# z on VectorE, earlier query normalizing, LN2 sums from accumulators and 640-wide evacuations in a gated mix of linear attention and a mixer MLP

## The chip, the cores and the metric

One Trainium2 chip, one of its cores. The metric is the device time of one execution in microseconds (us). The kernel before takes 268.58 us, median of the 4 runs timed beside the changed kernel (268.53 to 268.66). The profile's span, first to last instruction, is about 1.6 us shorter than that time: 267.0 us.

## The reference, cut to what matters

S = 2048 tokens, D = 640, 32 heads of 20, F = 1728, everything bf16.

```python
g = sigmoid((x * gate_w).sum(-1))
# A: linear attention
q, k, v = split(x @ wqkv); pq, pk = phi(q), phi(k)     # phi: t+1 if t>0 else exp(t); + 1e-6
kv  = einsum("bhsd,bhse->bhde", pk, v)
z   = pk.sum over tokens                               # [heads, 20] = 640 numbers
num = einsum("bhqd,bhde->bhqe", pq, kv)
den = einsum("bhqd,bhd->bhq", pq, z) + 1e-6
a   = (num / den) @ wo
# B: mixer
h   = gelu(layernorm(x) @ w1); hs = shift_by_quarter(h) @ w2
x1  = x + hs
b   = x1 + gelu(layernorm(x1) @ w3) @ w4
return g * a + (1 - g) * b
```

Of the kernel before, what the change touches and what calls it, by code (L numbers as in the profile page):

```python
# [50 lines left out]
class _Sched:  # L51
# [179 lines left out]
    def simulate(self):  # L231
        SEM_LAT = 60.0
        seq = self.seq
        while self.sim_pos < len(seq):
# [7 lines left out]
            if sem is not None and sem.startswith("d:") and nbytes < 0:  # L242
                self.eng_free[eng] = t + 1350.0
                end = t + 2800.0
                self.ev_time[(sem, val)] = end
            elif sem is not None and sem.startswith("d:"):
                self.eng_free[eng] = t + (500.0 if eng == "sp" else 1000.0)
                self.dma_free = max(self.dma_free, t) + nbytes / 330.0
                end = self.dma_free + 1900.0
                if self.ev_time.get((sem, val), 0.0) < end:  # L250
                    self.ev_time[(sem, val)] = end
            else:
                end = t + cost
                self.eng_free[eng] = end
                self.ev_time[(sem, val)] = end
# [169 lines left out]
def _build(nc, A_x, A_wqkv, A_wo, B_w1, B_w2, B_w3, B_w4, gate_w, out, dbg=None, stop=None):  # L425
# [55 lines left out]
    bn2 = pa.alloc("bn2", [128, NT, 2], F32)  # L481
    bns = pa.alloc("bns", [128, 4, 12], F32)
# [17 lines left out]
    zacc = pa.alloc("zacc", [128, D], F32)  # L500
# [12 lines left out]
    qprod = rb.alloc("qprod", [128, D], F32)  # L513
# [124 lines left out]
    def stt(out_ap, in0, scalar, in1, op0, op1):  # L638
        rd = [in0, in1] + ([scalar] if not isinstance(scalar, (int, float)) else [])
        n = nfree(out_ap)  # L640
        cost = (65.0 + n / 0.96) if (in_psum(in0) or in_psum(in1)) else (160.0 + 1.04 * n)
        return dve(lambda e: e.scalar_tensor_tensor(out_ap, in0, scalar, in1, op0, op1), rd, [out_ap], cost=cost)  # L642
# [81 lines left out]
    memset(pool, zacc[:], 0.0)  # L724
# [63 lines left out]
    def z_add(t):  # L788
        tt(pool, zacc[:, :] if t < NT - 1 else zsum[:, :], zacc[:, :], pk_tok[:, t, :], ALU.add)

    def ln_chunk_stats1(c):
        cs = slice(4 * c, 4 * c + 4)
        rs = lr[:, cs, 0:1].rearrange("p t o -> p (t o)")
        ts(pool, st1[:, 2, cs], rs, 1.0 / D, 0.0, ALU.mult, ALU.add)
        ts(pool, st1[:, 3, cs], st1[:, 1, cs], 1.0 / D, EPS_LN, ALU.mult, ALU.add)
        tt(pool, st1[:, 4, cs], st1[:, 2, cs], st1[:, 2, cs], ALU.mult)
        tt(pool, st1[:, 5, cs], st1[:, 3, cs], st1[:, 4, cs], ALU.subtract)
        tt(pool, st1[:, 6, cs], st1[:, 5, cs], negh[:, 0:4], ALU.pow)
        tt(pool, st1[:, 7, cs], st1[:, 2, cs], st1[:, 6, cs], ALU.mult)
        ts(pool, st1[:, 7, cs], st1[:, 7, cs], -1.0, 0.0, ALU.mult, ALU.add)  # L800
# [83 lines left out]
    def stats1(c):  # L884
        ln_chunk_stats1(c)
# [11 lines left out]
    for u in range(NT):  # L897
        IT.add("Z", ("z", u), 0.0, lambda u=u: z_add(u), deps=[(("n1", NT - 1), 0.0)] if u == 0 else [(("z", u - 1), 1.5)])
# [65 lines left out]
    for h in range(2):  # L964
# [3 lines left out]
    IT.add("KVF", ("zb",), 0.3, zb_group, deps=[(("z", NT - 1), 1.7)])  # L968
# [12 lines left out]
    def ln_chunk_stats2(c):  # L981
        cs = slice(4 * c, 4 * c + 4)
        mean = bn2[:, cs, 0:1].rearrange("p t o -> p (t o)")
        var = bn2[:, cs, 1:2].rearrange("p t o -> p (t o)")
        ts(pool, st2[:, 2, cs], var, 1.0, EPS_LN, ALU.mult, ALU.add)
        tt(pool, st2[:, 6, cs], st2[:, 2, cs], negh[:, 0:4], ALU.pow)
        tt(pool, st2[:, 7, cs], mean, st2[:, 6, cs], ALU.mult)
        ts(pool, st2[:, 7, cs], st2[:, 7, cs], -1.0, 0.0, ALU.mult, ALU.add)

    def w2_tile(t):  # L990
        tok = slice(2 + 128 * t, 2 + 128 * (t + 1))
        b1, b2 = bank(), bank()
        mm_group(ps[:, b1, 0:512], [(hsT[:, k, tok], w2[:, k, 0:512]) for k in range(KD)])
        mm_group(ps[:, b2, 0:128], [(hsT[:, k, tok], w2[:, k, 512:D]) for k in range(KD)])
        tt(dve, x_tok[:, t, 0:512], ps[:, b1, 0:512], x_tok[:, t, 0:512], ALU.add)
        tt(dve, x_tok[:, t, 512:D], ps[:, b2, 0:128], x_tok[:, t, 512:D], ALU.add)
        sb_ = slot("bns", 4)
        dve(lambda e: e.bn_stats(bns[:, sb_, 0:6], x_tok[:, t, 0:320]), [x_tok[:, t, 0:320]], [bns[:, sb_, 0:6]], cost=400.0)
        dve(lambda e: e.bn_stats(bns[:, sb_, 6:12], x_tok[:, t, 320:D]), [x_tok[:, t, 320:D]], [bns[:, sb_, 6:12]], cost=400.0)
        dve(lambda e: e.bn_aggr(bn2[:, t, :], bns[:, sb_, :]), [bns[:, sb_, :]], [bn2[:, t, :]], cost=110.0)  # L1000
        if t % 4 == 3:
            ln_chunk_stats2(t // 4)
# [43 lines left out]
    def a_tile(t):  # L1046
# [13 lines left out]
    def w4_half(t):  # L1060
# [21 lines left out]
    def w4_tile(t):  # L1082
# [20 lines left out]
        stt(x_tok[:, t, 0:512], ps[:, b1, 0:512], stg[:, 3, t:t + 1], abx[:, sa, 0:512], ALU.mult, ALU.add)  # L1103
        stt(x_tok[:, t, 512:D], ps[:, b2, 0:128], stg[:, 3, t:t + 1], abx[:, sa, 512:D], ALU.mult, ALU.add)
# [20 lines left out]
    for t in range(NT):  # L1125
# [95 lines left out]
```

## The kernel before: the parts that the change touches

The kernel is made by a small order-maker. Every piece of work is an item of a stream with dependencies; the order-maker keeps a model of each engine's time and always emits the item whose inputs it believes to be ready first. The emitted order is then fixed: on the chip each engine runs its list in order and waits on semaphores.

```python
# _Items.run(), cut: the choice of the next item
for d, lag in it["deps"]:
    if d not in done: ok = False; break
    v = done[d] + 100.0                       # modelled end of the dependency
    if v > est: est = v
key = (max(est, t_pe), 0 if it["dur"] == 0.0 else 1, -cp[n])
if best is None or key < best[0]: best = (key, n, s_)
```

The work runs in stages: q and k projections with phi (10 to 54 us in the profile), G = x^T pk (54 to 82), mixed with w1; then w1 and w2 (to 119), w3, and from 149 on `a` (normalized query times M), w3 and w4 mixed.

```python
def z_add(t):                                 # z: 16 adds on GpSimd
    tt(pool, zacc[:, :] if t < NT - 1 else zsum[:, :], zacc[:, :], pk_tok[:, t, :], ALU.add)

def zb_group():                               # z summed over partitions and broadcast, by TensorE
    b = pair()
    mm_group(ps[:, b, 0:512], [(ones_c[:, 0:128], zsum[:, 0:512])])
    mm_group(ps[:, b + 1, 0:128], [(ones_c[:, 0:128], zsum[:, 512:D])])
    copy(dve, zb[:, :], psf[:, 512 * b:512 * b + D])
# ...
for j in range(KD):
    IT.add("KVF", ("m", j), 0.57, lambda j=j: m_group(j), deps=...)
IT.add("KVF", ("zb",), 0.3, zb_group, deps=[(("z", NT - 1), 1.7)])   # behind the M groups

def w2_tile(t):                               # residual and LN2 statistics, cut
    tt(dve, x_tok[:, t, 0:512], ps[:, b1, 0:512], x_tok[:, t, 0:512], ALU.add)
    tt(dve, x_tok[:, t, 512:D], ps[:, b2, 0:128], x_tok[:, t, 512:D], ALU.add)
    # ... bn_stats twice, bn_aggr once, on VectorE

def qn_tile(t):                               # query normalizing, cut
    tt(dve, qprod[:, :], pq_tok[:, t, :], zb[:, :], ALU.mult)
    # tensor_reduce per head; + eps; reciprocal; multiply pq_tok by it; all on VectorE
    sch.dma("sp", pqnT[:, :, 128 * t:128 * (t + 1)], pq_tok[:, t, :], ..., transpose=True)
# ...
deps = [(("zb",), 1.0), (("q", max(t, 2)), 2.0), (("w2", NT - 1), 0.5)]
deps.append((("w3", 0, 3 * t), 0.0) if t < 4 else (("w4", t - 4), 0.0))
IT.add("QN", ("qn", t), 0.0, lambda t=t: qn_tile(t), deps)

def normalize(which, t, st):                  # LN1 and LN2, on GpSimd, three buffers xn
    ts(pool, xn[:, sx, :], x_tok[:, t, :], st[:, 6, t:t + 1], st[:, 7, t:t + 1], ALU.mult, ALU.add)
# then a DMA transpose xn -> xnT
```

## Time and profile before

| | us |
|---|---|
| time | 268.58 |
| span of the profile | 267.0 |
| PE busy | 259.9 |
| DVE (VectorE) busy | 154.2 |
| POOL (GpSimd) busy | 101.2 |
| ACT (ScalarE) busy | 95.1 |

The first part of the page, the kernel before. Each entry is busy time, share of the span, number of instructions.

```profile
PE 259.9 (97%) x1727; PEld 136.4 (51%) x1727; DVE 154.2 (58%) x308; ACT 95.1 (36%) x184; POOL 101.2 (38%) x153
```

TensorE is the bound: no other engine is above 58%. Next, the waits of PE in the kernel before (engine, line, what it waited for: us in total, times, longest).

```profile
PE ps L608 <- DMA pqnT<-pq_tok: 1.6, 1, 1.6
PE ps L827 <- POOL ones_c L662: 1.6, 1, 1.6
PE ps L850 <- DMA wq<-in_A_wqkv_dram: 0.7, 1, 0.7
PE ps L850 <- DVE xT L668: 0.4, 1, 0.4
```

Three of the four stand in the first 8 us. The one for pqnT is the only hole in the middle, and the chain that ended last shows what led to it (start, us, what; short pieces between them are left out):

```profile
161.54 1.08 DVE x_tok L642 x2
163.38 0.83 DVE dnr L1035
164.84 0.82 DVE pq_tok L1040
165.69 3.51 DMA pqnT<-pq_tok
```

A w4 tile is evacuated, then the query of the next tile is normalized by VectorE, then it is transposed by a DMA, and TensorE waits for that. Last, the timeline of VectorE around the G stage (start, busy us, line, operation, operands; in brackets the idle time before it), and the group of z adds on GpSimd (count, busy us, mean ns):

```profile
55.56 0.82 DVE L642 SCALAR_TENSOR_TENSOR pk_tok<-ps,Er 128x640 bf16<-128x640 f32 x1
82.38 1.09 DVE L636 TENSOR_TENSOR x_tok<-ps,x_tok 128x512 bf16<-128x512 f32 x2 [25.99 <-PE ps L608]
```

```profile
L636 POOL TENSOR_TENSOR zacc<-zacc,pk_tok 128x640 f32<-128x640 f32 x15 | 21.0, 1400 | 0.4
```

VectorE stands idle for 26 us in which z could be summed; GpSimd spreads the same sum from 79 to 137 us.

### The profile page before, as it was taken

How to read it: one execution, taken by the hardware profiler on the slowest of the kernel's cores; microseconds unless marked ns; L12 is line 12 of the kernel's file. 1: busy time of each engine (PE TensorE's matmuls, PEld its weight loads, DVE VectorE, ACT ScalarE, POOL GpSimd, SP SyncE). 2: the span in 40 equal slices, each digit the busy share in tenths (PEclk: the TensorE clock that was granted, in tenths of full speed). 3: DMA queues.
4: the chain of work that ended last, by engine and by line, in shares of the span. 5: the costliest groups of instructions: out<-in, count | busy, mean ns of one | idle time of the engine just before them, and what ended most of it. 6: DMA issues, size and time to landing. Idle time of an engine off the chain costs nothing.

```text
span 267.0 us, 4369 instructions
## 1 busy us (share of the span) xinstructions
PE 259.9 (97%) x1727; PEld 136.4 (51%) x1727; DVE 154.2 (58%) x308; ACT 95.1 (36%) x184; POOL 101.2 (38%) x153
## 2 busy tenths in 40 slices
PE   7899999999999999999999999799999999999995
PEld 3555555555454546554444555354544555545553
DVE  1597877830005667995009957879733753766533
ACT  1396677743443552614555300003322302130000
POOL 5003995756579294965950020210103010030200
PEclk9999999999999999999999999999999999999999
DMA  6755997647768211415369510411701121110411
GB/s 180 262 90 138 185 196 135 189 84 116 101 125 267 96 39 35 87 27 64 76 128 311 52 25 3 49 25 25 150 0 27 30 97 27 20 29 0 125 49 49
DMA packets 50292, 24.78 MB, mean 93 GB/s; under 512 B 41692, under 2 KB 48861, under 8 KB 50272
## 3 DMA queue, kind: packets, MB, share of 16 engines
q1 hardware_dynamic: 49120, 21.23, 36.1%
q0 software_dynamic: 1152, 3.28, 5.3%
q8 instruction: 13, 0.21, 0.4%
q14 instruction: 7, 0.06, 0.1%
HBM read 12.04 MB, written 2.62 MB: 55 GB/s over the span
## 4 chain that ended last, share of the span: by engine, by line
PE 93%; DMA 3%; DVE 2%; SPq 1%; issue 0%
PE ps L608 62%; PE ps L1096 20%; PE ps L778 8%; DMA wq<-in_A_wqkv_dram 2%; DMA pqnT<-pq_tok 1%; PE ps L1078 1%; PE ps L1026 1%; PE ps L850 1%; SPq L283 1%; PE ps L929 1%; DVE x_tok L642 1%; DVE dnr L1035 0%; DVE pq_tok L1040 0%; DVE qprod L636 0%; PE ps L619 0%
## 5 line engine op out<-in xcount | busy, mean ns | idle before, releaser
L659 ACT ACTIVATE h2T<-ps 128x512 bf16<-128x512 f32 x52 | 31.1, 597 | 84.4 <-PE ps L608 84.4
L1096 PE MATMUL ps<-w_86,h2T 128*128 128x512 bf16 (+1 forms) x416 | 58.9, 299 | 0.0
L608 PE MATMUL ps<-xnT,w_60 128*128 128x512 bf16 x260 | 58.7, 379 | 0.0
L630 POOL TENSOR_SCALAR abx<-x_tok,stg 128x640 f32<-128x640 bf16 x16 | 14.9, 935 | 109.1 <-DVE x_tok L642 60.0
L1096 PEld LDWEIGHTS ps<-w_86,h2T 128*128 128x128 bf16 x416 | 32.5, 98 | 27.6 <-issue 1.8
L608 PEld LDWEIGHTS ps<-xnT,w_60 128*128 128x128 bf16 x260 | 24.7, 98 | 27.5 <-DVE abx L642 0.3
L636 DVE TENSOR_TENSOR x_tok<-ps,x_tok 128x512 bf16<-128x512 f32 (+1 forms) x32 | 15.6, 486 | 33.7 <-PE ps L608 32.0
L642 DVE SCALAR_TENSOR_TENSOR x_tok<-ps,stg,abx 128x512 bf16<-128x512 f32 (+1 forms) x32 | 16.9, 548 | 31.2 <-PE ps L1096 31.2
L659 ACT ACTIVATE Er<-ps 128x640 bf16<-128x640 f32 x32 | 22.5, 705 | 19.2 <-PE ps L608 9.8
L659 ACT ACTIVATE hsT<-ps 128x512 bf16<-128x512 f32 (+1 forms) x32 | 18.9, 594 | 24.9 <-PE ps L608 24.5
L608 PE MATMUL ps<-M_sb,pqnT 128*128 128x512 bf16 (+1 forms) x160 | 23.9, 299 | 1.6 <-DMA pqnT<-pq_tok 1.6
L778 PE MATMUL ps<-pk_tok,x_tok 128*128 128x512 bf16 (+1 forms) x160 | 24.2, 299 | 0.0
L608 PE MATMUL ps<-wkg,xT 128*128 128x512 bf16 (+1 forms) x160 | 24.0, 299 | 0.0
L608 PE MATMUL ps<-w_62,hsT 128*128 128x512 bf16 (+1 forms) x160 | 23.9, 299 | 0.0
L608 PE MATMUL ps<-xnT,w_61 128*128 128x512 bf16 x100 | 23.9, 379 | 0.0
L642 DVE SCALAR_TENSOR_TENSOR abx<-ps,stg,abx 128x512 f32<-128x512 f32 (+1 forms) x32 | 17.5, 549 | 9.7 <-POOL abx L630 5.0
L636 POOL TENSOR_TENSOR zacc<-zacc,pk_tok 128x640 f32<-128x640 f32 x15 | 21.0, 1400 | 0.4
L608 PE MATMUL ps<-wq,xT 128*128 128x128 bf16 (+1 forms) x140 | 21.1, 299 | 0.0
L608 PEld LDWEIGHTS ps<-M_sb,pqnT 128*128 128x128 bf16 x160 | 12.9, 98 | 13.0 <-DMA pqnT<-pq_tok 1.8
L608 PEld LDWEIGHTS ps<-w_62,hsT 128*128 128x128 bf16 x160 | 13.1, 98 | 11.7
L608 PEld LDWEIGHTS ps<-wkg,xT 128*128 128x128 bf16 x160 | 12.9, 97 | 9.4
L778 PEld LDWEIGHTS ps<-pk_tok,x_tok 128*128 128x128 bf16 x160 | 12.6, 98 | 8.8
(70 smaller groups left out, 256.5 us busy)
## 6 DMA issues: line engine op xcount, KB each, us to landing
w_60<-in_B_w_dram SPq DMA_DIRECT2D x1, 2160.0 KB, 9.8
w_86<-in_B_w_dram SPq DMA_DIRECT2D x1, 2080.0 KB, 8.8
x_tok<-in_A_x_dram SPq DMA_DIRECT2D x3, 640.0 KB, 6.1
out_dram<-x_tok SPq DMA_DIRECT2D x3, 640.0 KB, 4.5
wq<-in_A_wqkv_dram SPq DMA_DIRECT2D x5, 160.0 KB, 4.7
wkg<-in_A_wqkv_dram SPq DMA_DIRECT2D x1, 800.0 KB, 7.5
wv<-in_A_wqkv_dram POOLq DMA_DIRECT2D x1, 800.0 KB, 5.4
wo_aug<-in_A_wo_dram POOLq DMA_DIRECT2D x5, 150.0 KB, 5.0
```

The source lines that it names most:

```text
L283: return e.dma_start(out_ap, in_ap)
L608: ins = e.matmul(out_ap, l, r, start=(i == 0), stop=(i == n - 1))
L630: return engf(lambda e: e.tensor_scalar(out_ap, in_ap, s1, s2, op0, op1), rd, [out_ap], cost=cost)
L636: return engf(lambda e: e.tensor_tensor(out_ap, a, b_, op), [a, b_], [out_ap], cost=cost)
L642: return dve(lambda e: e.scalar_tensor_tensor(out_ap, in0, scalar, in1, op0, op1), rd, [out_ap], cost=cost)
L659: return act(lambda e: e.activation(out_ap, in_ap, func, bias=bias, scale=scale), rd, wr, cost=cost)
L778: ins = e.matmul(o, l, r, start=(t0 + q_ == 0), stop=(t0 + q_ == NT - 1))
L850: ins = e.matmul(o, l, r, start=(k == 0), stop=(k == KD - 1))
L929: ins = e.matmul(o, l, r_, start=st_, stop=sp_, skip_group_check=True)
L1026: ins = e.matmul(o, l, r, start=st, stop=sp)
L1078: ins = e.matmul(o, l, r, start=True, stop=False)
L1096: ins = e.matmul(o, l, r, start=False, stop=(i == KFF - 1))
```

## The change

The intent: use VectorE's idle time for z, have zb 70 us earlier, and so move query normalizing ahead of and into the w1/w2 stage, where its result is ready long before `a` needs it. VectorE gets room for that by taking the LN2 sums from accumulators (the sum of x1 with the residual add, the sum of squares by ScalarE) and by evacuating 640 columns with one instruction, not 512 and 128 with two. The core of the diff, cuts marked:

```diff
-    def z_add(t):
-        tt(pool, zacc[:, :] if t < NT - 1 else zsum[:, :], zacc[:, :], pk_tok[:, t, :], ALU.add)
+    def z_sum(g):
+        cs = slice(160 * g, 160 * (g + 1))
+        dve(lambda e: e.tensor_reduce(qprod[:, cs], pk_tok[:, :, cs].rearrange("p n d -> p d n"), mybir.AxisListType.X, ALU.add),
+            [pk_tok[:, t, cs] for t in range(NT)], [qprod[:, cs]], cost=2740.0)
+        if g == 3:
+            copy(dve, zsum[:, :], qprod[:, :])
 ...
-    IT.add("KVF", ("zb",), 0.3, zb_group, deps=[(("z", NT - 1), 1.7)])
+    IT.add("ZB", ("zb",), 0.0, zb_group, deps=[(("z", 3), 1.7)])
 ... w2_tile: (the two bn_stats and the bn_aggr go)
-        tt(dve, x_tok[:, t, 0:512], ps[:, b1, 0:512], x_tok[:, t, 0:512], ALU.add)
-        tt(dve, x_tok[:, t, 512:D], ps[:, b2, 0:128], x_tok[:, t, 512:D], ALU.add)
+        stt(x_tok[:, t, :], psf[:, 512 * b:512 * b + D], 1.0, x_tok[:, t, :], ALU.mult, ALU.add, accum=st2[:, 0, t:t + 1])
+
+    def w2_sq(t):
+        activation(junk[:, 0, :], x_tok[:, t, :], ACTF.Square, accum=st2[:, 1, t:t + 1])
 ... qn_tile is cut into qn_sum, qn_scale and qt_tile (the transpose), and a_tile and w4_tile evacuate 640 columns in one
-        deps = [(("zb",), 1.0), (("q", max(t, 2)), 2.0), (("w2", NT - 1), 0.5)]
-        deps.append((("w3", 0, 3 * t), 0.0) if t < 4 else (("w4", t - 4), 0.0))
-        IT.add("QN", ("qn", t), 0.0, lambda t=t: qn_tile(t), deps)
+        deps = [(("zb",), 1.0), (("q", max(t, 2)), 2.0)]
+        if 3 <= t < 11:
+            i = (5 * (t - 3)) // 2 + 1
+            deps.append((("w1", i // KD, i % KD), 0.0))
+        elif t >= 11:
+            deps.append((("w3", 0, 2 * (t - 11)), 0.0))
+        IT.add("QN", ("qs", t), 0.0, lambda t=t: qn_sum(t), deps)
+        IT.add("QN", ("qn", t), 0.0, lambda t=t: qn_scale(t), [(("qs", t), 0.0)])
+        IT.add("QT", ("qt", t), 0.0, lambda t=t: qt_tile(t), deps=[(("qn", t), 3.2), (("w2", NT - 1), 0.5), (("t2", NT - 1), 0.0)])
```

One edit outside this cut matters in e9: the first of the two evacuations of Lt (the masked kv from which M is made) now comes before the second kv group in the order, and not behind it.

`pk_tok[:, :, cs].rearrange("p n d -> p d n")` reads 16 tokens' values of one column one after the other, and these lie 640 elements, 1280 bytes, apart. And zb is now a stream of its own with duration 0, so the order-maker puts it on TensorE as soon as it believes z to be done, with 2740 ns assumed for each reduction.

More of the change, by code (lines that the diff above doesn't have):

```diff
@@ L246, in simulate @@
             elif sem is not None and sem.startswith("d:"):
-                self.eng_free[eng] = t + (500.0 if eng == "sp" else 1000.0)
+                self.eng_free[eng] = t + (1000.0 if eng == "pool" else 500.0)
                 self.dma_free = max(self.dma_free, t) + nbytes / 330.0
@@ L480, in _build @@
     st2 = pa.alloc("st2", [128, 8, NT], F32)
-    bn2 = pa.alloc("bn2", [128, NT, 2], F32)
-    bns = pa.alloc("bns", [128, 4, 12], F32)
     stg = pa.alloc("stg", [128, 4, NT], F32)
@@ L499, in _build @@
     junk = pa.alloc("junk", [128, 1, D], BF16)
-    zacc = pa.alloc("zacc", [128, D], F32)
+    qprod = pa.alloc("qprod", [128, D], F32)
     zsum = pa.alloc("zsum", [128, D], BF16)
@@ L512, in _build @@
     abx = rb.alloc("abx", [128, 4, D], F32)
-    qprod = rb.alloc("qprod", [128, D], F32)
     sch.stats["sbuf"] = (pa.cur - pa.lo, pa.hi - pa.lo, ra.cur - ra.lo, rb.cur - rb.lo, ra.hi - ra.lo)
@@ L636, in tt, with stt @@
         return engf(lambda e: e.tensor_tensor(out_ap, a, b_, op), [a, b_], [out_ap], cost=cost)
-    def stt(out_ap, in0, scalar, in1, op0, op1):
+    def stt(out_ap, in0, scalar, in1, op0, op1, accum=None):
         rd = [in0, in1] + ([scalar] if not isinstance(scalar, (int, float)) else [])
@@ L641, in stt @@
         cost = (65.0 + n / 0.96) if (in_psum(in0) or in_psum(in1)) else (160.0 + 1.04 * n)
+        if accum is not None:
+            return dve(lambda e: e.scalar_tensor_tensor(out_ap, in0, scalar, in1, op0, op1, accum_out=accum), rd,
+                       [out_ap, accum], cost=cost + 70.0)
         return dve(lambda e: e.scalar_tensor_tensor(out_ap, in0, scalar, in1, op0, op1), rd, [out_ap], cost=cost)
@@ L723, in _build @@
     aselect(mask[0:120], mask_t[0:120], [[20, 6], [0, 20]], ALU.is_ge, 19, -1)
-    memset(pool, zacc[:], 0.0)
     memset(pool, Lt[:], 0.0)
@@ L786, in gt_step, with ln_chunk_stats @@
             activation(GT[:, i, :], psf[:, 512 * b:512 * b + D], ACTF.Copy)
-    def z_add(t):
-        tt(pool, zacc[:, :] if t < NT - 1 else zsum[:, :], zacc[:, :], pk_tok[:, t, :], ALU.add)
-    def ln_chunk_stats1(c):
-        cs = slice(4 * c, 4 * c + 4)
-        rs = lr[:, cs, 0:1].rearrange("p t o -> p (t o)")
-        ts(pool, st1[:, 2, cs], rs, 1.0 / D, 0.0, ALU.mult, ALU.add)
-        ts(pool, st1[:, 3, cs], st1[:, 1, cs], 1.0 / D, EPS_LN, ALU.mult, ALU.add)
-        tt(pool, st1[:, 4, cs], st1[:, 2, cs], st1[:, 2, cs], ALU.mult)
-        tt(pool, st1[:, 5, cs], st1[:, 3, cs], st1[:, 4, cs], ALU.subtract)
-        tt(pool, st1[:, 6, cs], st1[:, 5, cs], negh[:, 0:4], ALU.pow)
-        tt(pool, st1[:, 7, cs], st1[:, 2, cs], st1[:, 6, cs], ALU.mult)
-        ts(pool, st1[:, 7, cs], st1[:, 7, cs], -1.0, 0.0, ALU.mult, ALU.add)
+    def z_sum(g):
[4 more added lines that the diff above has]
+            copy(dve, zsum[:, :], qprod[:, :])
+    def ln_chunk_stats(st, c, rs):
+        cs = slice(4 * c, 4 * c + 4)
+        ts(pool, st[:, 2, cs], rs, 1.0 / D, 0.0, ALU.mult, ALU.add)
+        ts(pool, st[:, 3, cs], st[:, 1, cs], 1.0 / D, EPS_LN, ALU.mult, ALU.add)
+        tt(pool, st[:, 4, cs], st[:, 2, cs], st[:, 2, cs], ALU.mult)
+        tt(pool, st[:, 5, cs], st[:, 3, cs], st[:, 4, cs], ALU.subtract)
+        tt(pool, st[:, 6, cs], st[:, 5, cs], negh[:, 0:4], ALU.pow)
+        tt(pool, st[:, 7, cs], st[:, 2, cs], st[:, 6, cs], ALU.mult)
+        ts(pool, st[:, 7, cs], st[:, 7, cs], -1.0, 0.0, ALU.mult, ALU.add)
     def gate_chunk(c):
@@ L884, in stats1 @@
     def stats1(c):
-        ln_chunk_stats1(c)
+        ln_chunk_stats(st1, c, lr[:, 4 * c:4 * c + 4, 0:1].rearrange("p t o -> p (t o)"))
         gate_chunk(c)
@@ L896, in _build @@
         IT.add("T1", ("t1", u), 0.0, lambda u=u: t_xn(1, u), deps=[(("n1", u), 1.1)])
-    for u in range(NT):
-        IT.add("Z", ("z", u), 0.0, lambda u=u: z_add(u), deps=[(("n1", NT - 1), 0.0)] if u == 0 else [(("z", u - 1), 1.5)])
+    for g in range(4):
+        IT.add("Z", ("z", g), 0.0, lambda g=g: z_sum(g), deps=[(("k", NT - 1), 2.0)])
     LAST_EXP = ("k", NT - 1)
@@ L963, in _build @@
         IT.add("KVF", ("kvt", h), 1.2 - 0.6 * h, lambda h=h: kvt_group(h), deps=[(("g", KD - 1), 1.0)])
-    for h in range(2):
         IT.add("KVF", ("lt", h), 0.0, lambda h=h: lt_evac(h), deps=[(("kvt", h), 0.0)])
@@ L979, in w1_group @@
             activation(hsT[p0:p1, j, o0:o0 + 512], ps[p0:p1, b, :], ACTF.Gelu_apprx_tanh)
-    def ln_chunk_stats2(c):
-        cs = slice(4 * c, 4 * c + 4)
-        mean = bn2[:, cs, 0:1].rearrange("p t o -> p (t o)")
-        var = bn2[:, cs, 1:2].rearrange("p t o -> p (t o)")
-        ts(pool, st2[:, 2, cs], var, 1.0, EPS_LN, ALU.mult, ALU.add)
-        tt(pool, st2[:, 6, cs], st2[:, 2, cs], negh[:, 0:4], ALU.pow)
-        tt(pool, st2[:, 7, cs], mean, st2[:, 6, cs], ALU.mult)
-        ts(pool, st2[:, 7, cs], st2[:, 7, cs], -1.0, 0.0, ALU.mult, ALU.add)
     def w2_tile(t):
         tok = slice(2 + 128 * t, 2 + 128 * (t + 1))
-        b1, b2 = bank(), bank()
-        mm_group(ps[:, b1, 0:512], [(hsT[:, k, tok], w2[:, k, 0:512]) for k in range(KD)])
-        mm_group(ps[:, b2, 0:128], [(hsT[:, k, tok], w2[:, k, 512:D]) for k in range(KD)])
-        tt(dve, x_tok[:, t, 0:512], ps[:, b1, 0:512], x_tok[:, t, 0:512], ALU.add)
-        tt(dve, x_tok[:, t, 512:D], ps[:, b2, 0:128], x_tok[:, t, 512:D], ALU.add)
-        sb_ = slot("bns", 4)
-        dve(lambda e: e.bn_stats(bns[:, sb_, 0:6], x_tok[:, t, 0:320]), [x_tok[:, t, 0:320]], [bns[:, sb_, 0:6]], cost=400.0)
-        dve(lambda e: e.bn_stats(bns[:, sb_, 6:12], x_tok[:, t, 320:D]), [x_tok[:, t, 320:D]], [bns[:, sb_, 6:12]], cost=400.0)
-        dve(lambda e: e.bn_aggr(bn2[:, t, :], bns[:, sb_, :]), [bns[:, sb_, :]], [bn2[:, t, :]], cost=110.0)
-        if t % 4 == 3:
-            ln_chunk_stats2(t // 4)
+        b = pair()
+        mm_group(ps[:, b, 0:512], [(hsT[:, k, tok], w2[:, k, 0:512]) for k in range(KD)])
+        mm_group(ps[:, b + 1, 0:128], [(hsT[:, k, tok], w2[:, k, 512:D]) for k in range(KD)])
+        stt(x_tok[:, t, :], psf[:, 512 * b:512 * b + D], 1.0, x_tok[:, t, :], ALU.mult, ALU.add, accum=st2[:, 0, t:t + 1])
+    def w2_sq(t):
+        activation(junk[:, 0, :], x_tok[:, t, :], ACTF.Square, accum=st2[:, 1, t:t + 1])
     def w3_group(c, j):
@@ L1029, in w3_half, with qn_sum @@
         activation(h2h[:, sl, :], ps[:, b, 0:256], ACTF.Gelu_apprx_tanh)
-    def qn_tile(t):
+    qn_slot = {}
+    def qn_sum(t):
         sd = slot("dnr", 4)
-        pq3 = pq_tok[:, t, :].rearrange("p (h d) -> p h d", d=DH)
         tt(dve, qprod[:, :], pq_tok[:, t, :], zb[:, :], ALU.mult)
@@ L1037, in qn_tile, with qn_scale @@
             [qprod[:, :]], [dnr[:, 0, sd, :]], cost=820.0)
+        qn_slot[t] = sd
+    def qn_scale(t):
+        sd = qn_slot[t]
+        pq3 = pq_tok[:, t, :].rearrange("p (h d) -> p h d", d=DH)
         ts(dve, dnr[:, 0, sd, :], dnr[:, 0, sd, :], EPS_PHI, None, ALU.add, ALU.bypass)
@@ L1041, in qn_tile, with qt_tile @@
             [pq3, dnr[:, 1, sd, :]], [pq3], cost=900.0)
+    def qt_tile(t):
         sch.dma("sp", pqnT[:, :, 128 * t:128 * (t + 1)], pq_tok[:, t, :], "trn%d" % slot("trn", 4), transpose=True)
@@ L1051, in a_tile @@
         tok = slice(128 * t, 128 * (t + 1))
-        b1, b2 = bank(), bank()
-        mm_group(ps[:, b1, 0:512], [(pqnT[:, j, tok], M_sb[:, j, 0:512]) for j in range(KD)])
-        mm_group(ps[:, b2, 0:128], [(pqnT[:, j, tok], M_sb[:, j, 512:D]) for j in range(KD)])
-        stt(abx[:, sa, 0:512], ps[:, b1, 0:512], stg[:, 2, t:t + 1], abx[:, sa, 0:512], ALU.mult, ALU.add)
-        stt(abx[:, sa, 512:D], ps[:, b2, 0:128], stg[:, 2, t:t + 1], abx[:, sa, 512:D], ALU.mult, ALU.add)
+        b = pair()
+        mm_group(ps[:, b, 0:512], [(pqnT[:, j, tok], M_sb[:, j, 0:512]) for j in range(KD)])
+        mm_group(ps[:, b + 1, 0:128], [(pqnT[:, j, tok], M_sb[:, j, 512:D]) for j in range(KD)])
+        stt(abx[:, sa, :], psf[:, 512 * b:512 * b + D], stg[:, 2, t:t + 1], abx[:, sa, :], ALU.mult, ALU.add)
     w4_banks = {}
@@ L1063, in w4_half @@
         pr = (t % 4) // 2
-        bs = [bank() for _ in range(4)]
-        for i in range(4):
-            bank_hold.add(bs[i])
-        w4_banks[t] = (bs[0], bs[1])
-        w4_banks[t + 1] = (bs[2], bs[3])
+        bs = []
+        for i in range(2):
+            b = pair()
+            bs += [b, b + 1]
+            w4_banks[t + i] = (b, b + 1)
+        bank_hold.update(bs)
         jobs = []
@@ L1102, in w4_tile @@
         bank_hold.discard(b2)
-        stt(x_tok[:, t, 0:512], ps[:, b1, 0:512], stg[:, 3, t:t + 1], abx[:, sa, 0:512], ALU.mult, ALU.add)
-        stt(x_tok[:, t, 512:D], ps[:, b2, 0:128], stg[:, 3, t:t + 1], abx[:, sa, 512:D], ALU.mult, ALU.add)
+        if t == NT - 1:
+            stt(x_tok[:, t, 0:512], ps[:, b1, 0:512], stg[:, 3, t:t + 1], abx[:, sa, 0:512], ALU.mult, ALU.add)
+            stt(x_tok[:, t, 512:D], ps[:, b2, 0:128], stg[:, 3, t:t + 1], abx[:, sa, 512:D], ALU.mult, ALU.add)
+        else:
+            stt(x_tok[:, t, :], psf[:, 512 * b1:512 * b1 + D], stg[:, 3, t:t + 1], abx[:, sa, :], ALU.mult, ALU.add)
     def out_tiles(t0, t1):
@@ L1132, in _build @@
         IT.add("W2", ("w2", t), 1.33, lambda t=t: w2_tile(t), deps)
+        IT.add("SQ", ("sq", t), 0.0, lambda t=t: w2_sq(t), [(("w2", t), 1.0)])
+        if t % 4 == 3:
+            IT.add("S2", ("s2", c), 0.0, lambda c=c: ln_chunk_stats(st2, c, st2[:, 0, 4 * c:4 * c + 4]), [(("sq", t), 1.0)])
     for u in range(NT):
-        deps = [(("w2", 4 * (u // 4) + 3), 5.2 + 0.9 * (u % 4))]
+        deps = [(("s2", u // 4), 3.2 + 0.9 * (u % 4))]
         if u >= 3:
@@ L1141, in _build @@
     IT.add("MISC", ("w3load",), 0.0, w3_load, deps=[(("k", NT - 1), 0.0), (("t1", NT - 1), 0.0)])
-    IT.add("MISC", ("w4load",), 0.0, w4_load, deps=[(("kvt", 1), 0.0), (("t1", NT - 1), 0.0), (("z", NT - 1), 1.5)])
+    IT.add("MISC", ("w4load",), 0.0, w4_load, deps=[(("kvt", 1), 0.0), (("t1", NT - 1), 0.0), (("z", 3), 1.5)])
     for c in range(NCH):
@@ L1146, in _build @@
             if c == 0 and j == 0:
-                deps0 = [(("kvt", 1), 0.0), (("z", NT - 1), 1.5)]
+                deps0 = [(("kvt", 1), 0.0), (("z", 3), 1.5)]
             else:
@@ L1157, in _build @@
     for t in range(NT):
-        deps = [(("zb",), 1.0), (("q", max(t, 2)), 2.0), (("w2", NT - 1), 0.5)]
-        deps.append((("w3", 0, 3 * t), 0.0) if t < 4 else (("w4", t - 4), 0.0))
-        IT.add("QN", ("qn", t), 0.0, lambda t=t: qn_tile(t), deps)
+        deps = [(("zb",), 1.0), (("q", max(t, 2)), 2.0)]
[7 more added lines that the diff above has]
+        IT.add("QT", ("qt", t), 0.0, lambda t=t: qt_tile(t), deps=[(("qn", t), 3.2), (("w2", NT - 1), 0.5), (("t2", NT - 1), 0.0)])
     for t in range(NT):
         c = t // 4
-        deps = [(("qn", t), 5.0), (("w4load",), 0.0), (("m", KD - 1), 1.0)]
+        deps = [(("qt", t), 3.0), (("w4load",), 0.0), (("m", KD - 1), 1.0)]
         if t >= 4:
```

## The prediction

> **What bounds the kernel now.** TensorE. The page's first table has PE busy 259.9 of 267.0 us (97%), against DVE 154.2, POOL 101.2, ACT 95.1; the chain that ended last is 93% PE. Summing matmul columns at 2.4 GHz (estimate: a 512-column matmul starts every 216 ns in the trace) gives 254.3 us. The rest of the span I account for from start-to-start gaps between matmuls: 1.6 us before the first one, 3.1 us of warm-up and waiting for xT and wq at the start, 2.5 us of about 0.1 us at each change between full and half-array matmuls, 3.0 us after the last matmul starts, and one real hole. That hole, at 167.4, is the only mid-kernel entry in PE's list of waits: 1.6 us for pqnT, the transposed normalized query. Its chain is: DVE evacuates w4's tile, then multiply 0.82, reduce 0.82, add 0.18, reciprocal 0.35, multiply 0.82 (all late, in the w4 stage), then 3.5 us of DMA transpose.
>
> **What the change does, and what it is worth.**
> 1. z leaves POOL (16 adds of 1.40 us, spread from 79 to 136.6) for four VectorE reductions of 160x16 elements in the G stage, where the timeline shows DVE idle from 56.4 to 82.4. Estimate: 2.75 us each (slope 1.01 ns per element, from the 512- and 128-wide adds at 681 and 292 ns, plus 0.16), 11 us in all. None of it is on PE's path, and zb comes near 69 instead of 139.
> 2. Query normalizing, 3.06 us a tile and 49 us in all, moves from the w3/w4 stages to the w1/w2 stage and the start of w3. This removes the 1.6 us hole. Value about -1.6 us: all that can be gained there.
> 3. LN2 sums: each w2 tile now takes two adds, two statistics and one aggregate, 2.1 us; then one 640-wide op with a sum, about 1.0 us. DVE gets back about 17 us, ACT pays 16 squares of 0.74+0.2 = 15 us at 40% load. PE does not wait there now.
> 4. 640-wide evacuations: a pair 0.75+0.35 us (pitch 1.1) becomes 0.83. Saves about 4 us of DVE per 16 tiles, off the path; but evacuation starts later and needs aligned PSUM pairs.
>
> The large DVE and POOL savings buy nothing: PE keeps the same matmuls. Ceiling about -1.8 us. Against it: DVE nearly full from 69 to 124 (my sum is about 65 us of work for 55, so normalizing will run on into w3), late w2 evacuations, pair allocation: I allow +0.3 us.
>
> **Prediction: 267.2 us, 8 in 10 between 266.4 and 269.4.** Faster by over 2%: 0.02; within 2%: 0.89; slower: 0.09.
>
> **To see in the profile.** PE's wait for pqnT gone; PE busy still near 260, its share up to about 98%; DVE's z reductions 2.7 us each, ended before 69; POOL busy down by about 21 us; DVE down by about 10; DVE 7 to 9 tenths over w1/w2; no new wait of PE over 0.5 us.
>
> **What would make it wrong.** The z reduction reads bf16 at a 1280-byte step. The Trainium skill, "SBUF — State Buffer", section "Door 1: The DMA port swizzle", says that each access to a new 16-byte line pays a penalty; no run here shows it yet. PE's order is fixed when the program is made, so zb sits near 69 on PE: at twice the time a reduction, z ends 11 us later and PE stands still for most of that, about 277 us. Next: Square needing ACT table loads (1.28 us each; two in all now) beside the GELUs, or PE waiting on PSUM pairs behind normalizing.

## The result

| | before | changed |
|---|---|---|
| time, median, us | 268.58 | 278.18 (277.23 to 278.93) |
| ratio to before | 1 | 1.0355 (1.0323 to 1.0387) |
| span | 267.0 | 276.4 |
| mean granted TensorE clock | 1.000 | 0.988 |
| PE / DVE / POOL / ACT busy | 259.9 / 154.2 / 101.2 / 95.1 | 263.4 / 149.9 / 84.4 / 106.7 |

A ratio here and below is the mean time of one kernel's fast runs over the mean of the other's fast runs of the same rounds, so it is not quite the ratio of the medians quoted; the brackets are 95% intervals.

The page of the changed kernel, and the waits of its PE:

```profile
PE 263.4 (95%) x1727; PEld 136.9 (50%) x1727; DVE 149.9 (54%) x234; ACT 106.7 (39%) x216; POOL 84.4 (31%) x148
```

```profile
PE ps L605 <- DVE zsum L668: 5.8, 1, 5.8
PE ps L605 <- DMA pqnT<-pq_tok: 1.9, 1, 1.9
PE ps L829 <- POOL ones_c L662: 1.6, 1, 1.6
PE ps L605 <- ACT h2T L659: 0.7, 1, 0.7
```

The hole for pqnT did not go; it moved from 167 to 146 us. Above it stands a new and longer one, for zsum. VectorE's timeline in the changed kernel shows why:

```profile
55.84 0.82 DVE L642 SCALAR_TENSOR_TENSOR pk_tok<-ps,Er 128x640 bf16<-128x640 f32 x1
56.70 17.86 DVE L789 TENSOR_REDUCE qprod<-pk_tok 128x160 f32<-128x2560 bf16 x4
74.59 0.49 DVE L668 CAST zsum<-qprod 128x640 bf16<-128x640 f32 x1
75.90 0.82 DVE L668 CAST zb<-ps 128x640 bf16<-128x640 f32 x1 [0.81 <-PE ps L605]
```

Four reductions take 17.86 us, 4.47 each, not 2.74. TensorE, whose order has zb at 69 us, stands still until 75 (timeline of PE, changed kernel):

```profile
67.04 2.32 PE L605 MATMUL ps<-xnT,w_59 128*128 128x512 bf16 x10
75.14 0.71 PE L605 MATMUL ps<-zsum,ones_c 128*128 128x512 bf16 x2 [5.78 <-DVE zsum L668]
75.65 2.34 PE L605 MATMUL ps<-xnT,w_59 128*128 128x512 bf16 x5
77.78 2.15 PE L777 MATMUL ps<-pk_tok,x_tok 128*128 128x512 bf16 x10
```

Look at the third line as well: five matmuls take 2.34 us, where ten took 2.32 before the hole. The same stretch by windows (stretch in us: length, then busy time of each engine, then the granted clock):

```profile
67.00:69.00 2.00, 2.00 (x14) 0.92 (x11) 2.00 (x1) 0.60 (x1) 1.31 (x2) 1.00 1.48 95
69.00:75.00 6.00, 0.36 (x2) 0.00 (x0) 5.97 (x3) 0.60 (x1) 3.07 (x4) 0.77 0.58 109
75.00:79.00 4.00, 3.86 (x10) 1.45 (x11) 3.05 (x6) 0.60 (x1) 3.28 (x4) 0.50 0.66 126
```

After the hole TensorE works at half clock for 4 us. Where the 9.4 us of span went, from the starts of the matmuls (time from one start to the next, less the columns at 2.4 a ns, an estimate: a 512-column matmul starts every 216 ns in these traces): 5.95 for the hole at zb, 2.11 for the ten matmuls at half clock after it, 0.86 for a w2 tile that waits at 127.1 for a w3 evacuation on ScalarE (by its matmuls' operands most likely for its PSUM pair), and 0.25 because the new pqnT hole (2.06) is a little longer than the old (1.81). That is 9.2; the rest is spread thin.

Two more readings belong to the second hole. GpSimd's LN2 normalizing, first before, then changed (count | busy us, mean ns):

```profile
L630 POOL TENSOR_SCALAR xn<-x_tok,st_55 128x640 bf16<-128x640 bf16 x16 | 14.0, 883 | 0.0
```

```profile
L627 POOL TENSOR_SCALAR xn<-x_tok,st_55 128x640 bf16<-128x640 bf16 x16 | 17.9, 1129 | 7.1 <-DMA xnT<-xn 6.7
```

And the pieces of the chain ahead of the pqnT wait in the changed kernel:

```profile
126.27 7.34 DMA xnT<-xn
133.71 2.20 POOL xn L627
...
145.28 2.65 DMA pqnT<-pq_tok
147.98 4.77 PE ps L605 x25
```

One DMA transpose took 7.34 us to land, where most take 2.6, and one normalizing instruction 2.20 us, where before all took 0.87 to 0.89.

### The profile page after: what moved, and what is told of

Same layout as the page of the kernel before. It is cut to its first block, busy times and chain, and to the rows that moved or that the text cites. A ratio compares the mean times of both kernels' runs of the same rounds, so it can differ in the third digit from the quotient of the medians.

```text
span 276.4 us, 4323 instructions
## 1 busy us (share of the span) xinstructions
PE 263.4 (95%) x1727; PEld 136.9 (50%) x1727; DVE 149.9 (54%) x234; ACT 106.7 (39%) x216; POOL 84.4 (31%) x148
## 4 chain that ended last, share of the span: by engine, by line
PE 77%; DVE 8%; DMA 6%; POOL 4%; ACT 2%; SPq 1%; issue 1%; DVEq 0%; POOLq 0%
PE ps L605 50%; PE ps L1092 20%; DVE qprod L789 6%; DMA xnT<-xn 4%; PE ps L777 4%; POOL xn L627 2%; DMA wq<-in_A_wqkv_dram 2%; POOL st_55 L633 1%; PE ps L1074 1%; DMA pqnT<-pq_tok 1%; ACT hsT L659 1%; PE ps L1014 1%; PE ps L852 1%; SPq L283 1%; DVE x_tok L640 1%
## 5 line engine op out<-in xcount | busy, mean ns | idle before, releaser
L605 PE MATMUL ps<-xnT,w_58 128*128 128x512 bf16 x260 | 61.2, 379 | 0.0
L642 DVE SCALAR_TENSOR_TENSOR x_tok<-ps,stg,abx 128x640 bf16<-128x640 f32 (+2 forms) x17 | 14.3, 845 | 62.6 <-PE ps L1092 62.6
L627 POOL TENSOR_SCALAR abx<-x_tok,stg 128x640 f32<-128x640 bf16 x16 | 12.7, 798 | 110.4 <-DVE x_tok L642 99.6
L605 PEld LDWEIGHTS ps<-xnT,w_58 128*128 128x128 bf16 x260 | 24.0, 98 | 24.4 <-issue 1.0
L642 DVE SCALAR_TENSOR_TENSOR abx<-ps,stg,abx 128x640 f32<-128x640 f32 x16 | 14.1, 884 | 34.0 <-PE ps L605 30.0
L605 PE MATMUL ps<-xnT,w_59 128*128 128x512 bf16 x100 | 25.1, 392 | 0.0
L777 PE MATMUL ps<-pk_tok,x_tok 128*128 128x512 bf16 (+1 forms) x160 | 24.8, 304 | 0.0
L658 ACT ACTIVATE junk<-x_tok 128x640 bf16<-128x640 bf16 x32 | 23.6, 736 | 1.4 <-DVE x_tok L640 0.9
L627 POOL TENSOR_SCALAR xn<-x_tok,st_55 128x640 bf16<-128x640 bf16 x16 | 17.9, 1129 | 7.1 <-DMA xnT<-xn 6.7
L789 DVE TENSOR_REDUCE qprod<-pk_tok 128x160 f32<-128x2560 bf16 x4 | 17.9, 4528 | 0.0
```

The source lines that it names most:

```text
L605: ins = e.matmul(out_ap, l, r, start=(i == 0), stop=(i == n - 1))
L627: return engf(lambda e: e.tensor_scalar(out_ap, in_ap, s1, s2, op0, op1), rd, [out_ap], cost=cost)
L642: return dve(lambda e: e.scalar_tensor_tensor(out_ap, in0, scalar, in1, op0, op1), rd, [out_ap], cost=cost)
L658: return act(lambda e: e.activation(out_ap, in_ap, func, bias=bias, scale=scale, accum_out=accum), rd, wr, cost=cost)
L777: ins = e.matmul(o, l, r, start=(t0 + q_ == 0), stop=(t0 + q_ == NT - 1))
L789: dve(lambda e: e.tensor_reduce(qprod[:, cs], pk_tok[:, :, cs].rearrange("p n d -> p d n"), mybir.AxisListType.X, ALU.add), [pk_tok[:, t, ...
```

## Experiments

The theory after the result, A: the step of 1280 bytes makes the reductions slow, and zb, placed for a fast z, holds TensorE; the half clock follows from the hole. Rivals: B, such reductions are slow in bf16 or with short rows, whatever the step; C, the rest of the change costs the time. A smaller theory, D, for the pqnT hole: the w4 load delays the transposes. All kernels were compared with the kernel before on the same chip; its median there was 268.95 to 269.15 us, with runs from 268.3 to 270.6. One execution was slow, the one of e10 at 272.3 us; it is left out of the ratio, though not of the median. e4 was run once and is not in the table.

| run | median us | ratio to before | 95% interval |
|---|---|---|---|
| changed kernel | 278.18 | 1.0355 | 1.0323 to 1.0387 |
| e1, z reads adjacent elements | 269.9 | 1.0019 | 0.9989 to 1.0049 |
| e2, zb later | 270.36 | 1.0050 | 0.9996 to 1.0105 |
| e3, z on GpSimd, zb early | 276.44 | 1.0268 | 1.0229 to 1.0306 |
| e5, filler matmuls | 277.98 | 1.0303 | 1.0251 to 1.0355 |
| e6, zb later and w4 load later | 268.08 | 0.9969 | 0.9953 to 0.9984 |
| e7, z and zb as before | 267.24 | 0.9937 | 0.9920 to 0.9954 |
| e8, z as a tree | 270.76 | 1.0052 | 1.0024 to 1.0079 |
| e9, normalizing alone | 272.95 | 1.0142 | 1.0116 to 1.0168 |
| e10, changed kernel, zb behind M | 267.5 | 0.9950 | 0.9918 to 0.9982 |

### e1: z reads adjacent elements

```diff
-        dve(lambda e: e.tensor_reduce(qprod[:, cs], pk_tok[:, :, cs].rearrange("p n d -> p d n"), ...
+        src = pk_tok[:, 4 * g:4 * g + 4, :].rearrange("p n d -> p (n d)").rearrange("p (d n) -> p d n", n=16)
+        dve(lambda e: e.tensor_reduce(qprod[:, cs], src, ...
```

> Same instruction order on every engine as the changed kernel, but each z reduction reads 2560 adjacent bf16 elements instead of elements 1280 bytes apart (the result is wrong on purpose). Theory A (the step of the reads makes the reductions slow and zb holds TensorE): each reduction 2.7 to 2.8 us instead of 4.5, the wait of TensorE for zsum falls from 5.8 us to under 0.5, the half-speed matmuls after it go as well, time 269 to 271 us. Rival B (bf16 reductions with 16-element rows are slow whatever the step): still 4.5 us each, time 278. Rival C (z is fast but the loss lies elsewhere, in LN2 sums, pairs, early normalizing): reductions 2.75 us and time still over 274.

The group of z reductions in this run:

```profile
L790 DVE TENSOR_REDUCE qprod<-pk_tok 128x160 f32<-128x2560 bf16 x4 | 11.0, 2811 | 0.0
```

Same shape, type and number of elements, 2.81 us in place of 4.53 (mean durations), and the wait for zsum is gone from the list. The time falls by 3.2 per cent (1.0019 over 1.0355), to that of the kernel before; the hole and the half clock, 5.95 and 2.11 us of a span of 276.4, make 2.9 per cent. B falls: bf16 in 16-element rows takes 1.10 ns an element when the elements are adjacent, and 1.77 at the changed kernel's step. C falls as the main cause. The comparison with the reference passed in this run though z is wrong in it, so its tolerance doesn't check z; nothing here rests on that. What stays is a wait for pqnT of 1.8 us.

### e4: which step is slow

The four reductions are cut into eight, each with another step between its elements:

```diff
+            s = (1, 2, 4, 8, 16, 40, 80, 640)[i]
+                src = pk_tok[:, 2 * i:2 * i + 2, :].rearrange("p n d -> p (n d)").rearrange("p (b n r) -> p b r n", n=16, r=s)
```

> One look. The changed kernel with its four z reductions cut into eight of 80 outputs of 16 bf16 elements (1280 elements each), which read with a step of 1, 2, 4, 8, 16, 40, 80 and 640 elements (2 to 1280 bytes) in this order (wrong result on purpose). [...]If the slow reads come from touching a new 16-byte line at every element, as the Trainium skill states under SBUF cachelines: steps 1, 2, 4 at 1.5 us, steps 8 and more at about 2.4 us (4.53/2.81 times). If they come from the long step of 1280 bytes alone (rival): all but the last at 1.5 us.

The group view, taken once over each reduction, in the order of the steps (the last number before the second bar is its duration in ns):

```profile
L797 DVE TENSOR_REDUCE qprod<-pk_tok 128x80 f32<-128x1280 bf16 x1 | 1.5, 1486 | 0.0
L797 DVE TENSOR_REDUCE qprod<-pk_tok 128x80 f32<-128x1280 bf16 x1 | 1.5, 1476 | 0.0
L797 DVE TENSOR_REDUCE qprod<-pk_tok 128x80 f32<-128x1280 bf16 x1 | 1.5, 1476 | 0.0
L797 DVE TENSOR_REDUCE qprod<-pk_tok 128x80 f32<-128x1280 bf16 x1 | 2.5, 2453 | 0.0
L797 DVE TENSOR_REDUCE qprod<-pk_tok 128x80 f32<-128x1280 bf16 x1 | 2.5, 2467 | 0.0
L797 DVE TENSOR_REDUCE qprod<-pk_tok 128x80 f32<-128x1280 bf16 x1 | 2.8, 2809 | 0.0
L797 DVE TENSOR_REDUCE qprod<-pk_tok 128x80 f32<-128x1280 bf16 x1 | 2.6, 2623 | 0.0
L797 DVE TENSOR_REDUCE qprod<-pk_tok 128x80 f32<-128x1280 bf16 x1 | 2.3, 2291 | 0.0
```

The run's one time was 276.56 us; only durations within it are compared. The edge lies between a step of 8 bytes (1476 ns) and one of 16 (2453 ns); beyond it the cost is 1.55 to 1.9 times, and the 1280 bytes of the changed kernel are, at 2291 ns, the mildest of the slow ones. The Trainium skill, "SBUF — State Buffer", section "Door 1: The DMA port swizzle" (its box on cachelines is what the expectation means), says that SBUF has 16-byte lines and that two accesses must hit a line for full rate: the trace agrees, with 1476 ns at a step of 8 bytes, where two elements share such a line, and 2453 at 16, where none do. Steps between these two were not tried. The rival, that only a very long step is slow, falls.

### e2: only the assumed cost, so that zb comes later

```diff
-            [pk_tok[:, t, cs] for t in range(NT)], [qprod[:, cs]], cost=2740.0)
+            [pk_tok[:, t, cs] for t in range(NT)], [qprod[:, cs]], cost=4470.0)
```

> Only the cost that the order-maker assumes for one z reduction is changed, 2740 to 4470 ns, so that the two zb matmuls stand later in TensorE's order (after one more block of G and w1); the reductions stay at 4.5 us. If the loss is the place of zb in TensorE's fixed order (theory A): wait for zsum under 0.5 us, time 269 to 271 us, a correct result. If VectorE being busy 18 us with z, or the rest of the change, is what costs (rival C): time stays over 274 us.

The reductions are as slow as before, yet the wait for zsum is gone and the time is 270.36 us, 1.0050. One number in the order-maker was worth about 3 per cent. So it is not VectorE's 18 us that cost time, but where TensorE meets them. The reductions, and the longest wait of PE that is left after the first 8 us, in its profiled execution (the slowest of its four, 272.61 us; half clock follows this wait too, from 141.0 to 143.2):

```profile
L789 DVE TENSOR_REDUCE qprod<-pk_tok 128x160 f32<-128x2560 bf16 x4 | 18.0, 4562 | 0.0
```

```profile
PE ps L605 <- DMA pqnT<-pq_tok: 2.9, 1, 2.9
```

### e3: z back on GpSimd, zb still early

zb keeps its own stream; z goes back to the old sixteen adds, behind LN1's normalizing:

```diff
-    for g in range(4):
-        IT.add("Z", ("z", g), 0.0, lambda g=g: z_sum(g), deps=[(("k", NT - 1), 2.0)])
+    for u in range(NT):
+        IT.add("Z", ("z", u), 0.0, lambda u=u: z_add(u), deps=[(("n1", NT - 1), 0.0)] if u == 0 else [(("z", u - 1), 1.5)])
```

> The changed kernel with z back on GpSimd as 16 adds after the first normalizing; all else of the change kept (normalizing as early as zb allows, LN2 sums from accumulators, 640-wide evacuations). Theory A (z alone does the harm): 267.5 to 270.5 us, near the kernel before; zb comes near 135, so a wait for pqnT of 1 to 4 us is likely. Rival C (the other parts do the harm): over 274 us.

```profile
PE ps L605 <- POOL zsum L633: 7.4, 1, 7.4
```

This missed its expectation, and not because of C: I had left zb in its own stream, and the order-maker again put it on TensorE too early, at 121 us, while the adds end at 128.4. The run is a second case of the same fault with another engine, and says nothing about the rest of the change. Why the order-maker misjudged GpSimd there I did not follow up. e7 repeats it without the flaw.

### e5: useless work in the hole

```diff
+        def fill(e):
+            for _ in range(26):
+                ins = e.matmul(ps[:, b, :], ones_c[:, 0:128], ones_c[:, 128:640], start=True, stop=True)
+        pe(fill, [ones_c[:, 0:640]], [ps[:, b, :]], cost=0.0)      # in front of the two zb matmuls
```

> The changed kernel with 26 useless 512-column matmuls right in front of the zb matmuls, to fill TensorE's wait (5.6 us at 216 ns each). If the half-speed matmuls after the wait (428 ns for 512 columns, 2.0 us lost in all) come from TensorE having stood idle: zb and what follows run at 216 ns, the wait for zsum is under 0.6 us, time 1.7 to 2.3 us below the changed kernel, 276 us, though more work is done. If they come from something else at that moment: the time is unchanged, 278 us, or longer.

```profile
68.53 5.78 PE L964 MATMUL ps<-ones_c 128*128 128x512 bf16 x26
74.59 0.45 PE L605 MATMUL ps<-zsum,ones_c 128*128 128x512 bf16 x2 [0.28 <-DVE zsum L668]
74.87 1.24 PE L605 MATMUL ps<-xnT,w 128*128 128x512 bf16 x5
```

The same five matmuls that took 2.34 us now take 1.24, and the granted clock is 1.00 from 75 to 79, where it was 0.50. From the first zb matmul to the first of the KV group it is 40.35 us, where the changed kernel needs 42.27: the 1.9 us of half clock are gone, though more work is done. The half clock thus came from standing idle. The Trainium skill, "TensorE: Matmul & The Clock Gate", section "Part 1: The HAM clock gate", says that after an idle window of about 3.4 us the clock halves, and that it comes back after as long a busy one. In kind the traces agree: 5.8 us idle, then 3.9 us at half clock. In length they do not: half clock also followed waits of 2.0 (e8), 2.7 (e9) and 2.9 us (e2) in mid-kernel, and none followed those of 1.6 to 1.9 there (the kernel before, e4, e1, the changed kernel's second). The total shows the gain only in part and misses the expected 276 us: the ratio fell from 1.0355 to 1.0303, with intervals that overlap. In the profiled run the wait for pqnT grew from 1.9 to 4.0 us, and 1.3 us of half clock came on top. That execution took 279.18 us at a mean clock of 0.994, and one other 278.76 at the same clock; the two at 0.999 took 277.19 and 276.55. Why this wait grew was not tested.

### e6: theory D for the pqnT hole

e2, with the load of w4 issued after the first four pqnT transposes:

```diff
-... w4_load, deps=[(("kvt", 1), 0.0), (("t1", NT - 1), 0.0), (("z", 3), 1.5)])
+... w4_load, deps=[(("kvt", 1), 0.0), (("t1", NT - 1), 0.0), (("z", 3), 1.5), (("qt", 3), 0.0)])
-... deps=[(("qn", t), 3.2), (("w2", NT - 1), 0.5), (("t2", NT - 1), 0.0)])
+... deps=[(("qn", t), 3.2), (("w2", NT - 1), 0.5), (("t2", NT - 1), 0.0)] + ([(("w4load",), 0.0)] if t >= 4 else []))
```

> The kernel with zb late (z reductions costed at 4470 ns), and the load of w4 issued after the first four pqnT transposes instead of before the last eight xnT transposes. Theory D (the new hole at 137 to 141, where TensorE waits 1.8 to 4.0 us for pqnT, comes from the 2 MB load sharing the DMA queues with the xnT transposes, 7.3 us to landing instead of 2.6, which holds the three xn buffers and with them the whole queue of transposes): xnT transposes all at 2.6 to 2.8 us to landing, no wait for pqnT over 0.5 us, time 0.5 to 1.3 per cent below the kernel with zb late alone, 267 to 268.5 us on this chip. Rival (VectorE or GpSimd is what delays the transposes): the wait stays over 1.5 us.

The last eight xnT transposes now land after 2.6 to 3.6 us, not up to 7.9 as in e2, and the wait for pqnT is gone from the list; the ratio fell from 1.0050 to 0.9969. The longest wait of PE after the first 8 us is now this one:

```profile
PE ps L605 <- ACT h2T L659: 0.7, 1, 0.7
```

So the load does delay the transposes, and with it out of the way the hole goes. The order-maker had placed `a` as if the transposes always landed after 2.8 us. Two cautions. The edit also moves `a`, which waits for w4 in the order-maker: TensorE comes to it at 150.0 us, where in e2 it came at 138.1. As the first pqnT landed at 137.8 (141.0 in e2), it would have been in time at the old place as well, an estimate from these two traces. And the load alone doesn't make the hole, as e10 shows below; D is only half of it.

### e7: the rest of the change, without z and without the early zb

e3, and in addition zb behind the M groups, as before the change:

```diff
-    IT.add("ZB", ("zb",), 0.0, zb_group, deps=[(("z", NT - 1), 1.7)])
+    IT.add("KVF", ("zb",), 0.3, zb_group, deps=[(("z", NT - 1), 1.7)])
```

> The changed kernel with z back on GpSimd and the zb matmuls back behind the M groups, as before the change; the other parts (LN2 sums, 640-wide evacuations, normalizing split and as early as zb allows) stay. If those parts are harmless: no wait for zsum, 267.5 to 270 us, within 1 per cent of the kernel before. If they cost something by themselves: over 272 us.

```profile
PE 260.4 (98%) x1727; PEld 136.5 (51%) x1727; DVE 130.6 (49%) x229; ACT 107.1 (40%) x216; POOL 104.1 (39%) x165
```

The lowest median of all: 267.24 us, a span of 265.4, 0.63 per cent below the kernel before, and a little better than expected. The old hole is 0.3 us here. So the LN2 sums, the 640-wide evacuations and the freer normalizing are worth what the change was meant to bring, and need no early zb.

### e8: a fast z, meant to beat all

```diff
+        h = 8 >> g
+        a, b_ = (pk_tok[:, 0:8, :], pk_tok[:, 8:16, :]) if g == 0 else (zt[:, 0:h, :], zt[:, h:2 * h, :])
+        o = zt[:, 0:h, :] if g < 3 else zsum[:, :].unsqueeze(1)
+        dve(lambda e: e.tensor_tensor(o, a, b_, ALU.add), [a, b_], [o], cost=65.0 + h * D / 1.92)
```

with e6's place of the w4 load.

> A version meant to beat both: z as a tree of four VectorE adds of contiguous bf16 (8, 4, 2 and 1 tiles of 640), in the space of wq and Er, which are free by then, and w4 loaded after the first four pqnT transposes. Estimate from the trace if bf16 adds run at two elements a cycle: 2.8, 1.5, 0.8, 0.5 us, z done 6 us after the last pk tile instead of 18; if at one element a cycle, 5.5, 2.8, 1.5, 0.8, and zb is waited for about 4 us. With the first: no wait of TensorE over 0.5 us between 10 and 264 us, 266.5 to 268.5 us, 0.3 to 0.9 per cent faster than before.

z is indeed done in 5.7 us (the first add, 5120 elements out, takes 2.83), zb stands at 62.7 on TensorE with no wait, and yet the run missed its expectation and is slower than before, 1.0052:

```profile
69.48 2.77 PE L606 MATMUL ps<-xnT,w 128*128 128x512 bf16 x9 [1.96 <-DMA xnT<-xn]
```

This is w1 waiting for LN1's transposes, and from 70.7 to 74.2 us TensorE then works at half clock. GpSimd makes their input, and its timeline in this run shows what happened to it while VectorE ran the tree and then the first normalizing:

```profile
56.63 3.00 POOL L634 TENSOR_TENSOR st<-st 128x4 f32<-128x4 f32 x2
59.72 2.29 POOL L634 TENSOR_TENSOR st<-st,negh 128x4 f32<-128x4 f32 x1
63.12 3.17 POOL L628 TENSOR_SCALAR xn<-x_tok,st 128x640 bf16<-128x640 bf16 x3
```

The first two of these together take 0.48 us and the next 1.04 in the changed kernel at the same place; here they end within 0.1 us of the end of the tree's first add (59.6) and of its third (62.0). The Trainium skill, "SBUF — State Buffer", section "Who interferes with whom", says that a VectorE instruction with two SBUF inputs contends with a GpSimd instruction that reads SBUF, because the two share a read port, while `tensor_reduce` does not. The traces fit: in the changed kernel, the eleven xn instructions that run beside the slow reductions alone take 0.87 to 0.88 us, and those that fall on the two tensor_tensor multiplies of the normalizing take up to 2.2. A faster z bought a slower LN1: so I read these traces, but I removed this contention in no run by itself.

### e9: normalizing alone

The kernel before, with nothing but the split and freer normalizing (`qn_sum`, `qn_scale`, `qt_tile` and their dependencies) taken from the change:

```diff
-        deps = [(("zb",), 1.0), (("q", max(t, 2)), 2.0), (("w2", NT - 1), 0.5)]
-        deps.append((("w3", 0, 3 * t), 0.0) if t < 4 else (("w4", t - 4), 0.0))
-        IT.add("QN", ("qn", t), 0.0, lambda t=t: qn_tile(t), deps)
+        # ... the lines of the change for qs, qn and qt, as in the diff above
```

> The kernel before with one part of the change alone: normalizing split into sum, scale and transpose and no longer tied to the end of w4 tiles; z on GpSimd, zb behind the M groups, LN2 statistics and 512+128 evacuations as before. If letting normalizing run ahead is the whole gain of the good parts: no wait for pqnT over 0.5 us, 267.0 to 267.8 us, the same 0.6 per cent gain as the kernel with z and zb as before. If it needs the VectorE time that the LN2 sums and the 640-wide evacuations free: a wait for pqnT of over 1 us stays, 268 to 270 us.

```profile
PE ps L608 <- DMA pqnT<-pq_tok: 2.7, 1, 2.7
```

272.95 us, slower than before by 1.4 per cent, and beyond both expectations. Alone, the freer normalizing does harm: it and the evacuations fill VectorE (154.3 us busy, e7 has 130.6; the chain ahead of the hole runs through VectorE from 163.2 to 170.6), and in place of the old wait of 1.6 us at 167 stands one of 2.7 at 170, with slower clock after it (0.994 over the run). e7 differs from e9 in the LN2 sums, the 640-wide evacuations and the order of the Lt evacuations (e9 waits 0.6 us for Lt, e7 doesn't), and is 2 per cent faster. My reading of e7 was too short: those parts are no idle savings, they make the room that the freer normalizing needs. Which of them makes how much of it, no run shows.

### e10: the changed kernel with one edit

```diff
-    IT.add("ZB", ("zb",), 0.0, zb_group, deps=[(("z", 3), 1.7)])
+    IT.add("KVF", ("zb",), 0.3, zb_group, deps=[(("z", 3), 1.7)])
```

> The changed kernel with a single edit: the zb matmuls go back to the stream of the M groups, behind them, as before; z stays on VectorE with its slow reads of 4.5 us. Theory A (the slow reductions do harm only through the early place of zb in TensorE's order): no wait for zsum, 267.0 to 268.5 us, below the kernel before. If 18 us of VectorE in the G stage cost anything else: over 269 us. The place of the w4 load before the last eight xnT transposes may leave a wait of 1 to 2 us, then 268.5 to 269.5.

```profile
L789 DVE TENSOR_REDUCE qprod<-pk_tok 128x160 f32<-128x2560 bf16 x4 | 18.0, 4552 | 0.0
```

```profile
PE ps L605 <- DMA pqnT<-pq_tok: 0.2, 1, 0.2
```

267.5 us, 0.9950. z is on VectorE, as slow as ever (4.55 us a reduction), done at 74.8, and nobody waits for it, since zb runs at 128.3. Normalizing then starts only at 129.6, so the early normalizing that the change was made for is given up. This settles that the slow reductions did harm only through zb's place on TensorE, within the 0.3 per cent of these intervals. e7 and e10 both beat both kernels; their intervals overlap, so I name no winner.

The run also limits theory D. The load of w4 is as early as in e2 (issued at 115.0; 115.5 there), and the xnT transposes behind it take up to 7.5 us to land, yet TensorE waits only 0.2 us for pqnT. What differs is GpSimd: with normalizing so late, LN2's xn instructions after the load take 0.87 to 0.88 us but for one of 1.44, where e2 has 1.77 and 2.10 among them. So I read these traces: the hole at 146 us took both, the load and the slowed GpSimd, and taking either away is enough. No run changed GpSimd's speed alone.

## Why the prediction was wrong

- **What bounds the kernel, and how much there was to gain: right.** I put the ceiling at -1.8 us; e7, the good parts alone, has a span 1.6 us shorter than before.
- **The step that failed: "Estimate: 2.75 us each (slope 1.01 ns per element, from the 512- and 128-wide adds ...)".** The slope came from instructions that read adjacent elements, and I used it for reads 1280 bytes apart. The runs show 2.81 us adjacent (e1) and 4.53 at the changed kernel's step. From it followed "DVE's z reductions 2.7 us each, ended before 69", "zb comes near 69" and "None of it is on PE's path": the reductions ended at 74.6, zb ran at 75.1 and TensorE waited 5.8 us for it.
- **The mechanism was in the text, as the first way to be wrong**: a penalty for each new 16-byte line, zb's fixed place, "about 277 us". I gave all that could make it slower 0.09, though neither my 2.75 us nor the 2740 ns in the diff had been measured at this step. The 277 was partly luck. I assumed reductions twice as slow and counted no half clock; they were 1.6 times as slow, and 2.1 us of half clock came on top.
- **Half clock after a hole: missing.** Measured 2.11 us (e5 gave 1.9 back).
- **"This removes the 1.6 us hole": wrong for the changed kernel, right for e6, e7 and e10.** The hole reappeared at 146 us because the w4 load, no longer held back by z on GpSimd, ran into the xnT transposes (e6) while GpSimd was slowed beside the early normalizing (e10, which has the load and not the hole).
- **"The large DVE and POOL savings buy nothing": wrong for DVE.** Without its savings the freer normalizing costs 1.4 per cent (e9), with them it gains 0.6 (e7). For POOL nothing speaks against it: e7 gives that saving up (104.1 us busy) and is as fast as e10 (83.3).
- **Smaller ones.** POOL fell by 16.8 us, not 21: its LN2 normalizing took 3.9 us more, beside the two-input multiplies, and the LN2 statistics about 3. DVE fell by 4.3, not 10: z took 7 us more. Square caused no table loads (two in all, as before). I allowed 0.3 us for PSUM pairs and late evacuations; the one such wait cost 0.86.

## What to carry to other kernels

When work moves to an idle engine, ask not only whether it fits there, but what on the bounding engine is ordered behind it, and give that a place with slack: e10 keeps the slow z and still beats both kernels. Cost an access by its pattern, not by its element count: for a bf16 reduction the edge was between 8 and 16 bytes of step. A hole on TensorE of 2.0 us or more cost more than its length in these traces, for half clock followed it, and savings on an engine off the path can be what lets another part of the same change work, so test the parts in combination as well as alone.

## What the Trainium skill lacked or had wrong

- "SBUF — State Buffer", section "Door 1: The DMA port swizzle": it says that one can stride for free up to 8 bf16 elements. Here a step of 8 elements (16 bytes) cost 2453 ns against 1476 for steps of 2 and 4; only its other sentence, two hits for each line, fits. It gives no size for the penalty: here 1.55 to 1.9 times for a VectorE bf16 reduction, largest at a step of 80 bytes.
- "VectorE: DVE Perf Modes": its table gives `tensor_reduce` one element a cycle, at its 0.96 GHz an estimate of 2667 ns for 2560, which adjacent elements come near (2811), but says nothing of the step: at 1280 bytes the same reduction took 4528 ns on average.
- "SBUF — State Buffer", section "Who interferes with whom": right in kind, but it doesn't say what several two-input VectorE instructions in a row do to a short GpSimd one: here one of 0.88 us took 2.1 to 2.2 us beside two multiplies of 0.8 to 1.2 us.
- How long TensorE must stand idle before its clock halves, by its page and by these traces (2.0 us and more), is compared under e5.
